# Two attention layers and two linear-attention layers on one core: another rule for TensorE's order, a one-product bias, and DMA transposes for the left-over rows

## The chip, the cores and the metric

The kernel runs on one core of a Trainium2 chip, in one launch. The time is the device time of one execution, in microseconds. A profile holds one execution, taken by the hardware profiler. Engines are TensorE (PE; its weight loads are listed as PEld), VectorE (DVE), ScalarE (ACT), GpSimd (POOL) and SyncE (SP), which here issues every DMA.

## The reference

Four blocks follow each other on x (1 x 2048 x 512): A, B, A, B, each added to its input after a layer norm.

```python
# A: 32 heads of 128, 8 memory rows, segments of 32 rows, one after the other
for s in range(n_seg):
    h = concat([mem, xs])                    # 8 + 32 = 40 rows
    q, k, v = h @ Wq, h @ Wk, h @ Wv
    p = softmax(where(mask, q @ k.T * scale, -1e9))
    o = (p @ v) @ Wo
    mem = o[:, :8]                           # feeds the next segment
    outs.append(o[:, 8:])
# B: 32 heads of 16, linear attention
pq, pk = phi(q), phi(k)                      # phi(t) = where(t > 0, t + 1, exp(t)) + 1e-6
o = (pq @ (pk.T @ v)) / (pq @ sum(pk) + 1e-6)
out = o @ wo
```

The mask lets every row see the 8 memory rows, and a row of the segment see the rows up to its own. A block of type A has 64 segments in a chain: the memory that leaves one segment enters the next.

## The kernel before, in words

All weights of A lie in SBUF from the start: Wq, Wk, Wv (512 x 4096) and Wo, 4 MB each. Working buffers lie in one tile, the arena, which A and B layers use in turn.

**How a segment is tiled.** The 40 rows of a segment are cut: a block of 32 rows holds the 8 memory rows and the segment's first 24 rows. The last 8 rows of four segments together make one more block of 32 rows, the left-over block of a group of four (`left_block`), and it doesn't depend on the memory. `project` multiplies a block by a weight: the block's 32 rows are the stationary side, so four matmuls stand side by side in TensorE's columns (tile form 128 x 32), each with 512 columns of the weight, four heads at once; four rounds over the 512 inputs. One PSUM bank then holds 16 heads (`b` is the half of the heads) in the layout "rows x head width". Values are used like that. Queries and keys are needed the other way round: `transposed` copies the bank to an image in SBUF (`img`, four slots), makes four transposes on TensorE (line 646, tile form 128 x 128) and copies the result to `qT` or `kT`, for the left-over block to `qTl` or `kTl`.

**The chain of a segment.** `mem_attention` (the memory's 8 queries against all 40 rows) starts its PSUM bank with a bias, the product of two constant tables `u16` and `w16` (line 701; 16 rows and 2 x 128 columns, tile form 16 x 128), adds the scores (710), takes the exponential (717), the sums (722), and the products with the values (735, 736), which are normalised into `oTb` (739). `out_block` multiplies by Wo (808, tile form 128 x 32 again) into `outW`, and `next_mem` brings the 8 memory rows back to the next segment's block (827). `x_attention` does the other 32 rows of the segment (759 scores, 763 exponential, 771 and 772 sums, 774 to 782, 792 and 793 values) and has until the next segment's `out_block`. `residual` adds the result to x (842, 847, 850). `prepare` makes the layer norm and the left-over block of the next group.

**What sets the order.** Nothing is issued as the functions are written. `P.add` records each operation with its cost, what it reads and writes, and its PSUM tile. `P.schedule`, once for each layer, walks a planned clock of each engine and picks, among the operations that are ready at that time, the one with the longest planned path to the layer's end (`tail`). Copies out of PSUM may go to ACT or DVE, whichever is planned to end first. For TensorE there are two further rules. Operations have a `mode` (`full`, `col` for the tile form 128 x 32, `bias`); among ready ones PE takes one of the mode that it is in, as long as its tail is at most MODE_SLACK (0.3) shorter than the longest. And a PSUM tile that isn't urgent starts only while three of the eight banks are free. Each engine then executes its own list in that order, and waits on semaphores for the others.

**B layers.** For each of 16 row tiles: layer norm, the three projections (914, 921), phi (898 to 901), the sums over all rows (937); then for each tile the numerator and denominator (956, 962), the quotient (967 to 971), transposes (979), the output projection (988) and the addition to x (991). Their two weights are loaded when the A layer has ended.

Of the kernel before, what the change touches and what calls it, by code (L numbers as in the profile page):

```python
# [18 lines left out]
MODE_SLACK = 0.3  # L19
# [35 lines left out]
class _Node:  # L55
    __slots__ = ("engs", "fn", "cost", "sync", "order", "tiles", "dsem", "dval", "eng", "start", "done",
                 "tail", "sig", "val", "waits", "know", "idx", "succ", "nleft", "urgent", "mode")


class _Prog:  # L60
# [17 lines left out]
    def add(self, engs, fn, cost, reads=(), writes=(), tiles=(), dsem=None, urgent=False, mode="full",  # L78
            after=()):
        nd = _Node()  # L80
        nd.mode = mode
        nd.engs = (engs,) if isinstance(engs, str) else tuple(engs)
# [41 lines left out]
    def schedule(self):  # L124
# [15 lines left out]
        for nd in reversed(nodes):  # L140
# [6 lines left out]
            nd.tail = best + min(nd.cost.values())  # L147
# [13 lines left out]
        n_left = len(nodes)  # L161
        pend = {e: [] for e in ENGINES}
# [25 lines left out]
        def n_free(t_now):  # L188
            k = 0
            for own in self.bank_owner:  # L190
                if own is None or (own.ops[-1].done is not None and own.ops[-1].done <= t_now):
                    k += 1
            return k
# [3 lines left out]
        def pick_for(e):  # L197
            tn = self.now[e]
            while pend[e] and pend[e][0][0] <= tn + EPS:
                _, _, nd = heapq.heappop(pend[e])  # L200
                if nd.done is None:
                    heapq.heappush(ready[e], (-nd.tail, nd.idx, nd))
            pick = None
            kept = []
            while ready[e]:
# [4 lines left out]
                if first_of(nd):  # L210
                    bf = bank_for(tn)
                    if bf is None or bf[1] > tn + EPS or (not nd.urgent and n_free(tn) < 3):
                        kept.append(item)
                        continue
# [10 lines left out]
                elif nd.tail < pick.tail - MODE_SLACK:  # L225
# [12 lines left out]
        while n_left:  # L238
# [47 lines left out]
            nd.done = nd.start + nd.cost[e]  # L286
            self.now[e] = nd.done - (0.09 if e == "act" else 0.05 if e == "dve" else 0.0)
# [94 lines left out]
def _build_kernel(nc, A_x, A_mem0, A_Wq, A_Wk, A_Wv, A_Wo, A_seg_len, B_wqkv, B_wo, out):  # L382
# [35 lines left out]
    w16_sb = sb("w16_sb", [128, 4, 2, 32])  # L418
# [31 lines left out]
    img = av(NI * 512).rearrange("p (r x) -> p r x", r=NI)  # L450
# [14 lines left out]
    xlnA = av(D).rearrange("p (r x) -> p r x", r=1)  # L465

# [73 lines left out]

    BIG = -1.0e9
    pool(lambda g: g.memset(w16_sb[:, :, 0, :], 0.0), ["w16"])
    pool(lambda g: g.memset(w16_sb[:, :, 1, :], BIG), ["w16"])
    for gg in range(4):
        a = w16_sb[:, gg, 0, :]
        sel(a, GE, BIG, 0, [[-4, 4], [0, 8]], 1, "w16")
        sel(a, GE, BIG, 3, [[4, 4], [0, 8]], -1, "w16")
        sel(w16_sb[:, gg, 1, :], ALU.not_equal, 0.0, -gg, [[-4, 4], [0, 8]], 1, "w16")
# [71 lines left out]
    def a_layer(layer):  # L620
        img_no = [0]
# [14 lines left out]
        def transposed(W, key, blk, bkeys, b, dst, dkey, urgent):  # L636

            tl = project(W, key, blk, bkeys, b, urgent)
            k = img_no[0] % NI
            img_no[0] += 1  # L640
# [11 lines left out]

        def left_block(G):
# [3 lines left out]
            for b in range(2):  # L657
                hs = slice(4 * b, 4 * b + 4)
                transposed(Wq_sb, "Wq", blk, bk, b, qTl[:, r2, hs, :, :], ("qTl", r2, b), False)
# [385 lines left out]
```

## Time and profile before

| | |
|---|---|
| runs, median (lowest to highest) | 2161.87 us (2161.3 to 2163.71) |
| profiled execution, its own time | 2159.93 us |
| mean granted TensorE clock | 0.994 |
| line 630, projections: matmuls | 15360 |
| line 808, output projection: matmuls | 5184 |
| ACT, copies out of PSUM and others on line 498 | 673.2 us in 1410 |
| DVE, the same on line 499 | 312.3 us in 541 (casts), 205.8 us in 543 (copies) |
| HBM over the span | 12 GB/s |

Times are in microseconds, of one entry in nanoseconds. "PE" is the engine's matmuls, "PEld" the loads of stationary tiles, which overlap them. A row of the order of time begins with the start and the duration of a run of like instructions; in brackets stands the idle time before it on its engine and what ended it. A matmul's end is modelled and overlaps the next one's start, so on TensorE the distance from start to start is the time that something takes. A stretch's row has its bounds, its length, and for each engine the busy time and the number of instructions, then the granted clock, the DMA engines' share and their GB/s.

### The profile page before, as it was taken

The numbers are of one execution on the slowest core, as the hardware profiler recorded it, in microseconds if no ns is written. First come the engines' busy times: TensorE is split into PE (matmuls) and PEld (weight loads), VectorE is DVE, ScalarE is ACT, GpSimd is POOL, SyncE is SP. The second block draws the span as 40 slices with busy tenths as digits, with TensorE's granted clock in tenths as the row PEclk, the third lists the DMA queues.
The fourth block names the chain that finished last, engine by engine and source line by source line (L and its number), as shares of the span: only waits on it lengthen the run. The fifth ranks groups of instructions, "written<-read, shape, count | busy, mean of one in ns | idle before, by whom it ended". The sixth has DMA issues, their size and how long they took to land.

```text
span 2158.2 us, 83024 instructions
## 1 busy us (share of the span) xinstructions
PE 2079.3 (96%) x37982; PEld 1163.5 (54%) x37982; DVE 1201.2 (56%) x3287; ACT 1159.7 (54%) x3112; POOL 14.8 (1%) x74
## 2 busy tenths in 40 slices
PE   1999999999999999998999999999999999999989
PEld 0555555555555555554655555555555555555545
DVE  0655555555554555556876555555555555554678
ACT  0555555555555555554645555555555555555554
POOL 2000000000000000000000000000000000000000
PEclk9999999999999999999999999999999999999999
DMA  9000000000000000001000000000000000000011
GB/s 350 3 3 2 3 3 3 3 3 3 3 3 3 3 3 3 3 3 41 1 2 3 3 3 3 3 2 3 3 3 3 3 3 3 3 3 3 3 41 40
DMA packets 12558, 30.48 MB, mean 14 GB/s; under 512 B 424, under 2 KB 9648, under 8 KB 10672
## 3 DMA queue, kind: packets, MB, share of 16 engines
q1 hardware_dynamic: 12208, 25.18, 3.2%
q8 instruction: 297, 4.87, 0.9%
q14 instruction: 53, 0.43, 0.1%
HBM read 23.08 MB, written 2.10 MB: 12 GB/s over the span
## 4 chain that ended last, share of the span: by engine, by line
PE 94%; DVE 2%; DMA 2%; ACT 1%; issue 0%; SPq 0%
PE pb L630 42%; PE pb L808 14%; PE pb L646 8%; PE pb L792 4%; PE pb L827 3%; PE pb L921 3%; PE pb L710 3%; PE pb L701 3%; PE pb L842 2%; PE pb L722 2%; DMA x_sb<-in_A_x_dram 2%; PE pb L735 2%; PE pb L759 2%; PE pb L914 1%; PE pb L736 1%; PE pb L771 1%
## 5 line engine op out<-in xcount | busy, mean ns | idle before, releaser
L498 ACT ACTIVATE arena_sb<-pb 128x512 bf16<-128x512 f32 (+6 forms) x1410 | 673.2, 492 | 458.7 <-PE pb L630 269.7
L630 PE MATMUL pb<-Wq_sb,arena_sb 128*32 128x512 bf16 x5120 | 478.2, 383 | 0.9 <-ACT arena_sb L498 0.4
L630 PE MATMUL pb<-Wk_sb,arena_sb 128*32 128x512 bf16 x5120 | 472.5, 382 | 0.0
L499 DVE CAST arena_sb<-pb 128x512 bf16<-128x512 f32 (+2 forms) x541 | 312.3, 578 | 237.6 <-PE pb L793 142.5
L630 PE MATMUL pb<-Wv_sb,arena_sb 128*32 128x512 bf16 x5120 | 374.4, 383 | 0.0
L808 PE MATMUL pb<-Wo_sb,arena_sb 128*32 128x512 bf16 x5184 | 350.1, 381 | 0.0
L780 DVE TENSOR_TENSOR arena_sb<-arena_sb 32x256 bf16<-32x256 bf16 x512 | 213.3, 417 | 133.6 <-ACT arena_sb L776 121.7
L499 DVE COPY arena_sb<-pb 128x512 bf16<-128x512 bf16 (+1 forms) x543 | 205.8, 399 | 137.8 <-PE pb L646 134.3
L646 PE MATMUL pb<-id_sb,arena_sb 128*128 128x128 bf16 x2560 | 216.7, 220 | 0.0
L630 PEld LDWEIGHTS pb<-Wq_sb,arena_sb 128*32 128x32 bf16 x5120 | 134.4, 96 | 133.2 <-ACT arena_sb L498 14.6
L646 PEld LDWEIGHTS pb<-id_sb,arena_sb 128*128 128x128 bf16 x2560 | 145.0, 97 | 103.2 <-issue 41.6
L630 PEld LDWEIGHTS pb<-Wk_sb,arena_sb 128*32 128x32 bf16 x5120 | 134.6, 97 | 108.5 <-issue 2.5
L717 ACT ACTIVATE arena_sb<-pb 128x256 bf16<-128x256 f32 x256 | 97.5, 381 | 158.9 <-PE pb L710 158.8
L498 ACT ACTIVATE outW_sb<-pb 128x256 fp32r<-128x256 f32 x198 | 75.8, 383 | 195.9 <-PE pb L808 194.5
L808 PEld LDWEIGHTS pb<-Wo_sb,arena_sb 128*32 128x32 bf16 x5184 | 119.7, 95 | 102.4 <-issue 20.7
L630 PEld LDWEIGHTS pb<-Wv_sb,arena_sb 128*32 128x32 bf16 x5120 | 109.6, 95 | 76.9
L782 DVE TENSOR_TENSOR arena_sb<-arena_sb 32x64 bf16<-32x64 bf16 x512 | 111.0, 217 | 15.8
L792 PE MATMUL pb<-arena_sb 128*128 128x128 bf16 x1024 | 115.2, 218 | 4.0 <-DVE arena_sb L782 4.0
L710 PE MATMUL pb<-arena_sb 128*128 128x32 bf16 x2048 | 118.6, 177 | 0.0
L499 DVE COPY arena_sb<-arena_sb 128x128 bf16<-128x128 bf16 x192 | 35.9, 194 | 128.8 <-PE pb L759 127.8
L793 PE MATMUL pb<-arena_sb 128*128 128x32 bf16 x1024 | 105.6, 178 | 0.0
L827 PEld LDWEIGHTS pb<-selm_sb,outW_sb 128*128 128x128 f32 x504 | 77.6, 188 | 51.8 <-ACT outW_sb L498 18.2
(108 smaller groups left out, 2330.6 us busy)
## 6 DMA issues: line engine op xcount, KB each, us to landing
Wq_sb<-in_A_Wq_dram SPq DMA_DIRECT2D x1, 4096.0 KB, 12.4
Wk_sb<-in_A_Wk_dram SPq DMA_DIRECT2D x1, 4096.0 KB, 22.2
Wv_sb<-in_A_Wv_dram SPq DMA_DIRECT2D x1, 4096.0 KB, 31.7
Wo_sb<-in_A_Wo_dram SPq DMA_DIRECT2D x1, 4096.0 KB, 43.2
arena_sb<-in_B_wqkv_dram SPq DMA_DIRECT2D x2, 1536.0 KB, 6.5
out_dram<-x_sb SPq DMA_DIRECT2D x16, 128.0 KB, 1.7
x_sb<-in_A_x_dram SPq DMA_DIRECT2D x1, 1920.0 KB, 11.5
arena_sb<-in_B_wo_dram SPq DMA_DIRECT2D x2, 512.0 KB, 7.5
```

The lines of the kernel that those rows point to most:

```text
L498: return e.activation(o() if callable(o) else o, i() if callable(i) else i, ACTF.Copy)
L499: return e.tensor_copy(o() if callable(o) else o, i() if callable(i) else i)
L630: r = pe.matmul(tl.f32()[32 * j:32 * j + 32, 0:512], blk[:, c, :], W[:, c, o:o + 512], start=(c == 0), stop=(c == 3), tile_position=(0, 32 ...
L646: r = pe.transpose(tt.bf16()[:, 128 * i:128 * i + 128], img[:, k, 128 * i:128 * i + 128], id_sb[:, :])
L710: r = pe.matmul(tl.f32()[:, o:o + 32], kk[:, hh, :, :].rearrange("p j x -> p (j x)"), qT[:, r2, hh, :, 0:8], start=False, stop=True, skip_ ...
L717: add("act", lambda a: a.activation(Pm[:, k, :, :].rearrange("p a q -> p (a q)"), tl.f32()[:, 0:256], ACTF.Exp, scale=SCALE), c_act(256), ...
L780: add("dve", lambda v, q=q, j=j: v.tensor_tensor(Pbx[q, :, j, 0:32], Px[q, :, :], Rx[q, :, :], ALU.mult), c_dve(256), reads=["Px", "Rx"], ...
L782: add("dve", lambda v, q=q, j=j: v.tensor_tensor(Pbx[q, :, j, 32:40], PLL[q, g2, :, gl], Rx[q, :, 24:32], ALU.mult), c_dve(64), reads=[("P ...
L792: pe.matmul(o, vimg[:, r2, e], Pbx[:, hh, :, 0:32], start=True, stop=False)
L793: return pe.matmul(o[:, :, 24:32], vleft[:, g2, e], Pbx[:, hh, :, 32:40], start=False, stop=True)
L808: r = pe.matmul(tl.f32()[32 * j:32 * j + 32, :], oT[:, 4 * hh + j, :], Wo_sb[:, 8 * j + hh, :], start=(hh == 0), stop=(hh == 7), tile_posi ...
L827: r = pe.matmul(tl.f32()[:, 8 * c:8 * c + 8], outW[:, s % 3, 128 * c:128 * c + 128], selm_sb[:, :], start=True, stop=True)
```

## The change

Four things change together.

1. **The planner's rules.** MODE_SLACK goes from 0.3 to 2.0. The picking key becomes `prio`: the tail, raised to that of the matmul ahead of it on the same PSUM tile while that one is still to come. A PSUM tile may start when more than two banks are free, more than one if it is urgent, and any if it is the oldest that hasn't started; a bank counts as free only with the lag after its last reader. Planned costs of lines 827, 842 and 847 (of before) rise. An operation may have a latency `lat` beyond its engine's time.
2. **The bias.** One product over all 128 rows of `u16` and 256 columns takes the place of two over 16 rows; its rows beyond 16 are zero in `u16`. `w16` is four times as wide, lies in the arena, and is filled by GpSimd at the start of each A layer. The mode `bias` is gone.
3. **The left-over rows.** `left_block` calls `turned` for queries and keys: the projection and the copy to an image stay, and SP issues a DMA transpose from the image to `qTl` or `kTl`. The four transposes on TensorE and the copy out of PSUM behind them are gone. These images have two slots of their own (4 and 5).
4. **Line numbers.** 630 becomes 639, 646 655, 701 717, 710 725, 722 737, 735 and 736 750 and 751, 739 754, 759 774, 771 786, 792 and 793 807 and 808, 808 823, 827 842, 842 857, 498 and 499 516 and 517.

```diff
-MODE_SLACK = 0.3
+MODE_SLACK = 2.0
...
-            nd.tail = best + min(nd.cost.values())
+            nd.tail = best + min(nd.cost.values()) + nd.lat
+        for nd in nodes:
+            nd.prio = nd.tail
+            for tl in nd.tiles:
+                k = tl.ops.index(nd)
+                if k and tl.ops[k - 1] in nd.order and tl.ops[k - 1].done is None:
+                    nd.prio = max(nd.prio, tl.ops[k - 1].prio)
...
-                    if bf is None or bf[1] > tn + EPS or (not nd.urgent and n_free(tn) < 3):
+                    while tiles[oldest[0]].bank is not None:
+                        oldest[0] += 1
+                    spare = 0 if tiles[oldest[0]] in nd.tiles else 1 if nd.urgent else 2
+                    if bf is None or bf[1] > tn + EPS or n_free(tn + EPS) <= spare:
...
-                elif nd.tail < pick.tail - MODE_SLACK:
+                elif nd.prio < pick.prio - MODE_SLACK:
...
-    img = av(NI * 512).rearrange("p (r x) -> p r x", r=NI)
+    img = av((NI + 2) * 512).rearrange("p (r x) -> p r x", r=NI + 2)
...
+        def turned(W, key, blk, bkeys, b, dst, dkey):
+            tl = project(W, key, blk, bkeys, b, False)
+            k = NI + img_no[1] % 2
+            img_no[1] += 1
+            evac(img[:, k, :], lambda: tl.f32()[:, :], 512, tiles=[tl], writes=[("img", k)])
+            add("sp", lambda e: e.dma_start_transpose(dst.rearrange("p h j x -> p h (j x)"), img[:, k, :]), 0.1,
+                reads=[("img", k)], writes=[dkey], dsem="turn%d" % k, lat=3.0)
...
-                transposed(Wq_sb, "Wq", blk, bk, b, qTl[:, r2, hs, :, :], ("qTl", r2, b), False)
-                transposed(Wk_sb, "Wk", blk, bk, b, kTl[:, r2, hs, :, :], ("kTl", r2, b), False)
+                turned(Wq_sb, "Wq", blk, bk, b, qTl[:, r2, hs, :, :], ("qTl", r2, b))
+                turned(Wk_sb, "Wk", blk, bk, b, kTl[:, r2, hs, :, :], ("kTl", r2, b))
...
-            def bias(pe):
-                for a in range(2):
-                    r = pe.matmul(tl.f32()[:, 128 * a:128 * a + 128], u16_sb[0:16, :],
-                                  w16_sb[0:16, g, a, :].unsqueeze(1).to_broadcast([16, 4, 32]), start=(a == 0),
-                                  stop=False, skip_group_check=True)
-                return r
-            add("pe", bias, c_pe(2, 128), reads=["u16", "w16"], tiles=[tl], urgent=True, after=early, mode="bias")
+            add("pe", lambda pe: pe.matmul(tl.f32()[:, 0:256], u16_sb[:, :],
+                                           w16_sb[:, g, :, :, :].rearrange("p a h x -> p (a h x)"), start=True,
+                                           stop=False, skip_group_check=True),
+                c_pe(1, 256), reads=["u16", "w16"], tiles=[tl], urgent=True, after=early)
```

**Where the order moves.** Three places show it.

The first is PE in the steady state of an A layer, from the last keys of a segment on. Names are outputs and inputs, `pb` is PSUM, then the output's size; 32x512 and 32x32 are matmuls of the tile form 128 x 32. Before:

```order
L630 MATMUL pb<-Wk_sb,arena_sb 32x512 x16
L646 MATMUL pb<-id_sb,arena_sb 128x128 x8
L630 MATMUL pb<-Wq_sb,arena_sb 32x512 x4
L630 MATMUL pb<-Wv_sb,arena_sb 32x512 x12
L701 MATMUL pb<-w_sb,u_sb 128x128 x2
L646 MATMUL pb<-id_sb,arena_sb 128x128 x4
L710 MATMUL pb<-arena_sb 128x32 x8
L630 MATMUL pb<-Wv_sb,arena_sb 32x512 x4
L630 MATMUL pb<-Wk_sb,arena_sb 32x512 x4
L646 MATMUL pb<-id_sb,arena_sb 128x128 x4
L722 MATMUL pb<-arena_sb,one_sb 128x128 x2
L630 MATMUL pb<-Wq_sb,arena_sb 32x512 x4
```

and now, from the same place on:

```order
L639 MATMUL pb<-Wk_sb,arena_sb 32x512 x16
L639 MATMUL pb<-Wv_sb,arena_sb 32x512 x32
L655 MATMUL pb<-id_sb,arena_sb 128x128 x8
L717 MATMUL pb<-arena_sb,u_sb 128x256
L655 MATMUL pb<-id_sb,arena_sb 128x128 x8
L725 MATMUL pb<-arena_sb 128x32 x4
L717 MATMUL pb<-arena_sb,u_sb 128x256
L807 MATMUL pb<-arena_sb 128x128
L808 MATMUL pb<-arena_sb 128x4x8
L725 MATMUL pb<-arena_sb 128x32 x4
```

The values' projection stands in one piece ahead of the transposes, and the tile form changes once in the lower list and seven times in the upper one. Over the whole program it changes 2278 times before and 1228 times after, 34 and 14 of them in each stretch from the last segment's end of an A layer through the B layer behind it.

The second is SP's queue at the start. Before:

```order
L512 DMA Wq_sb<-in_A_Wq_dram 128x4x4096
L512 DMA Wk_sb<-in_A_Wk_dram 128x4x4096
L512 DMA Wv_sb<-in_A_Wv_dram 128x4x4096
L513 DMA Wo_sb<-in_A_Wo_dram 128x32x512
L509 DMA x_sb<-in_A_x_dram 128x512
L510 DMA arena_sb<-in_A_mem_dram 8x512
L514 DMA x_sb<-in_A_x_dram 128x15x512
```

and now:

```order
L530 DMA Wk_sb<-in_A_Wk_dram 128x4x4096
L530 DMA Wq_sb<-in_A_Wq_dram 128x4x4096
L527 DMA x_sb<-in_A_x_dram 128x512
L530 DMA Wv_sb<-in_A_Wv_dram 128x4x4096
L531 DMA Wo_sb<-in_A_Wo_dram 128x32x512
L668 DMA_TRANSPOSE arena_sb<-arena_sb 128x4x128
L528 DMA arena_sb<-in_A_mem_dram 8x512
L668 DMA_TRANSPOSE arena_sb<-arena_sb 128x4x128
L532 DMA x_sb<-in_A_x_dram 128x15x512
L668 DMA_TRANSPOSE arena_sb<-arena_sb 128x4x128 x62
```

The first tile of x comes ahead of Wv and Wo, the memory rows come behind the first transpose, and the rest of x behind the second; all transposes of the layer follow.

The third is ACT's list in the steady state of after, with the semaphores that each instruction waits for (`s_turn5` is the landing of a transpose from image slot 5):

```order
L742 ACTIVATE arena_sb<-arena_sb 128x128 [waits s_act]
L516 ACTIVATE arena_sb<-pb 128x512 [waits s_turn5,s_pe]
L516 ACTIVATE outW_sb<-pb 128x256 [waits s_pe]
L778 ACTIVATE arena_sb<-pb 128x256 [waits s_pe]
L516 ACTIVATE outW_sb<-pb 128x256 [waits s_act]
```

The second row is the copy of a left-over image into slot 5, which waits for the transpose that read the slot before; the evacuation of `outW`, which the next segment's memory needs, is queued behind it. Before, such a copy waited for PE alone.

49 lines of the change are left out of this document (28 added, 21 removed).

## The prediction

> **What bounds the kernel now.** I read the page first: the span, the engines' shares, the granted clock and the chain that ended last. Then the busy times by stage, then the order of time on TensorE.
>
> ```profile
> span 2158.2 us, 83024 instructions
> PE 2079.3 (96%) x37982; PEld 1163.5 (54%) x37982; DVE 1201.2 (56%) x3287; ACT 1159.7 (54%) x3112; POOL 14.8 (1%) x74
> PEclk9999999999999999999999999999999999999999
> PE 94%; DVE 2%; DMA 2%; ACT 1%; issue 0%; SPq 0%
> ```
>
> The profiled execution took 2159.93 us, the median of the three runs is 2161.87, so 1.9 us separate them. VectorE and ScalarE are a little over half busy and the clock is full. TensorE is on the chain for 94%. Its busy time alone proves little, because the ends of matmuls are modelled. The stages come next: stretch, length, then the busy time of PE, PEld, DVE, ACT, POOL.
>
> ```profile
> 49.00:992.00 943.00, 943.00 (x17899) 521.81 (x17899) 509.79 (x1413) 523.19 (x1424) 0.00 (x0) 1.00 0.01 3
> 992.00:1126.00 134.00, 117.86 (x1473) 71.25 (x1472) 102.08 (x260) 67.48 (x168) 0.21 (x2) 0.94 0.05 17
> ```
>
> The first stretch is the first A layer: PE has no gap in it. The second is the B layer with a segment at either end: there PE does wait (16 us). What PE does while "busy" is seen in the order of time, where the starts, not the ends, are to be read (start, duration, line):
>
> ```profile
> 502.36 1.04 PE L630 MATMUL pb<-Wq_sb,arena_sb 128*32 128x512 bf16 x16
> 503.22 1.04 PE L630 MATMUL pb<-Wk_sb,arena_sb 128*32 128x512 bf16 x16
> 504.19 0.62 PE L646 MATMUL pb<-id_sb,arena_sb 128*128 128x128 bf16 x8
> 504.74 0.40 PE L630 MATMUL pb<-Wq_sb,arena_sb 128*32 128x512 bf16 x4
> 504.97 0.82 PE L630 MATMUL pb<-Wv_sb,arena_sb 128*32 128x512 bf16 x12
> 505.73 0.28 PE L701 MATMUL pb<-w_sb,u_sb 16*128 16x128 bf16 x2
> 505.94 0.40 PE L646 MATMUL pb<-id_sb,arena_sb 128*128 128x128 bf16 x4
> 506.17 0.35 PE L710 MATMUL pb<-arena_sb 128*128 128x32 bf16 x8
> 506.46 0.40 PE L630 MATMUL pb<-Wv_sb,arena_sb 128*32 128x512 bf16 x4
> 506.68 0.39 PE L630 MATMUL pb<-Wk_sb,arena_sb 128*32 128x512 bf16 x4
> 507.00 0.40 PE L646 MATMUL pb<-id_sb,arena_sb 128*128 128x128 bf16 x4
> ```
>
> Sixteen column-tiled matmuls (128*32 weights, four side by side) take 503.22 - 502.36 = 0.86 us, so one group of four takes 0.215. Four transposes take 506.17 - 505.94 = 0.23, or 0.057 each, and the same 128*128 form follows them with no extra. Wherever the form changes there is an extra: 503.22 to 504.19 is 0.97 for 0.86 of work (0.11); 504.19 to 504.74 is 0.55 for 0.45 (0.10); 504.97 to 505.73 is 0.76 for 0.645 (0.11); 505.73 to 505.94, two products of the 16-row form, is 0.21 for 0.11 (0.10); 506.68 to 507.00 is 0.32 for 0.215 (0.10). **A change of tile form costs PE about 0.10 us**, and every start stands where the one before lets it. Counted over the whole program of before, the form changes 2278 times: 228 us.
>
> ```profile
> 514.73 0.76 PE L827 MATMUL pb<-selm_sb,outW_sb 128*128 128x8 f32 x4
> 574.62 0.75 PE L827 MATMUL pb<-selm_sb,outW_sb 128*128 128x8 f32 x4
> ```
>
> These two are the same matmul, four segments apart: 59.9 us. Adding up that stretch of the program at such intervals (0.215 a group, 0.057 a transpose, 0.026 for 32 columns and so on) gives 52.2 us of matmuls, and 72 changes at 0.10 add 7.2: 59.4. Real waiting is some 0.5 us in 60. So in the A layers time is TensorE's work plus its form changes.
>
> [...]
>
> **The change part by part.**
>
> *Form changes.* With MODE_SLACK 2.0, the wish to finish a tile, and a bias product of 128 rows in place of a 16-row form, the program of after changes form 1228 times: 1050 fewer, at 0.10 us **105 us**. All but 40 of them are in the A layers. The 40 are in the B layers, where PE waits anyway: I count their 4 us as not gained.
>
> *Transposes.* 2560 become 2048; 512 at 0.057 are **29 us** of PE. With them go 128 of these copies out of PSUM, 0.42 or 0.60 us each, on engines that are not the bound, so I count nothing for them:
>
> ```profile
> L646 PE MATMUL pb<-id_sb,arena_sb 128*128 128x128 bf16 x2560 | 216.7, 220 | 0.0
> L499 DVE COPY arena_sb<-pb 128x512 bf16<-128x512 bf16 x491 | 195.4, 420 | 136.0 <-PE pb L646 134.3
> L498 ACT ACTIVATE arena_sb<-pb 128x512 bf16<-128x512 bf16 x213 | 125.9, 597 | 41.3 <-PE pb L979 30.6 <-PE pb L646 10.8
> ```
>
> *Bias.* Two products of 128 columns (0.11) become one of 256:
>
> ```profile
> 499.95 0.28 PE L771 MATMUL pb<-arena_sb,bo_sb 128*128 128x256 bf16 x1
> 500.07 0.19 PE L772 MATMUL pb<-arena_sb,bo_sb 128*128 128x64 bf16 x1
> ```
>
> That is 0.12: no gain beyond the form changes already counted. Its table is now filled on GpSimd at each A layer's start, 14 instructions of 0.3 to 0.5 us by the rows below, some 5 us, while the first projections and transposes of that layer (about 10 us of PE work) run ahead of the first bias. Uncovered it would cost 5 us once.
>
> ```profile
> L524 POOL TENSOR_SCALAR_AFFINE_SELECT id_sb<-id_sb 128x128 bf16<-128x128 bf16 x1 | 0.3, 292 | 0.2 <-POOL id_sb L528 0.2
> L559 POOL MEMSET arena_sb<- 128x480 bf16 x1 | 0.5, 498 | 0.1
> ```
>
> *The DMA transposes.* 128 of them, 128 KB each, on SP, which does nothing else in an A layer. Each begins when its image has been copied from PSUM. In the steady state two kinds of instruction wait for one: the copy that refills the same image slot, and the copies and scores that read the result. Counting PE work between an image's last matmul and the waiting place, less the image's own copy (0.25 to start, 0.6 to run), the cover is about 3.4 us at three places in eight segments, about 4.5 at one, and 9 to 38 elsewhere: 48 and 16 places in the kernel. Behind the waiting copy on ACT stands the evacuation of outW, the recurrence itself. No row shows a DMA transpose. The nearest are
>
> ```profile
> out_dram<-x_sb SPq DMA_DIRECT2D x16, 128.0 KB, 1.7
> arena_sb<-in_B_wo_dram SPq DMA_DIRECT2D x2, 512.0 KB, 7.5
> ```
>
> Same size 1.7 us; the longest that does not queue behind the 16 MB of weights 7.5. I take the first, with room up to 3.4: **nothing**. At 7.5 it would be 48 x 4.1 + 16 x 3.0 = 245 us.
>
> [...]
>
> *Start.* SP's queue now has x's first tile third instead of fifth:
>
> ```profile
> 9.87 29.62 SPq L509 DMA_DIRECT2D x_sb<-in_A_x_dram  x1
> 45.96 0.69 DVE L601 BATCH_NORM_STATS2 st_sb<-x_sb 128x6 f32<-128x512 bf16 x1 [22.66 <-DMA x_sb<-in_A_x_dram]
> 48.48 0.26 PE L588 MATMUL pb<-id_sb,arena_sb 8*128 8x8 bf16 x4
> Wk_sb<-in_A_Wk_dram SPq DMA_DIRECT2D x1, 4096.0 KB, 22.2
> ```
>
> It waited 30 us for room behind Wo. Behind two weights it should land near 24 us, and the first left-over block (24 groups x 0.215 = 5.2 us) runs while Wv and Wo load. The first transpose now takes the blocked place and the memory rows (L588) follow it, so segment 0 begins near 47 to 50 us as now. I take **-6 us**, between +3 and -9.
>
> *New waits.* With PE's work shorter, the copies that it waits for have less to hide behind.
>
> ```profile
> 504.67 0.76 DVE L499 COPY arena_sb<-pb 128x512 bf16<-128x512 bf16 x2
> ```
>
> This copy starts 0.25 us after the first four of the transposes at 504.19 are through (504.42) and takes half of 0.76 when two follow each other, 0.42 alone: 0.67 us. In the order of after, between four L655 and the L725 that needs their copy stand four more (0.23), a bias (0.12) and eight (0.46): 0.81. Such places, with less than 0.1 us left once release and queue are counted, are some 18 in four segments, against some 11 before, and at one (L823 behind the product L754) about 0.4 us is missing. I take 1.1 us of waiting for four segments in place of 0.5, over 32 such stretches **+20 us**; from 0 to +105 (all the form changes given back).
>
> Sum: 2159.9 - 105 - 29 + 4 - 6 + 20 = 2044; with half of the difference to the median, **2045 us**.
>
> **Rivals.**
>
> 1. *A DMA transpose outlasts its cover.* For it: slot and reader wait in order, and 1.7 us is of a plain copy. Against: 3.4 us is twice that. At 4.2 us it costs 48 x 0.8 = 38 (2083), at 5 us 48 x 1.6 + 16 x 0.5 = 85 (2130).
> 2. *The same, beyond 5.5 us: slower than before.* There 48 x 2.1 + 16 x 1.0 = 117 eats the whole gain; at 6.5 us it is 48 x 3.1 + 16 x 2.0 = 181, 2225 us. ACT's idle 46% could soften it, since not all of its delay reaches PE.
> 3. *The longer runs of one form starve the recurrence.* Copies wait longer for a whole tile, and the saved changes come back as gaps before L655, L725 and L842: half gives 2097, all 2150. Against: 0.5 us of waits in 60 now, and a chain through one segment of some 10 us by the same rows (16 groups 3.4, transposes and copies 1.5, exponential to product 2, output projection 0.9 to 1.7, two copies and L827 1.2) under 13.8 us of PE work for one.
> 4. *PE is not the bound*, so nothing changes: 2155 to 2160. The starts speak against it.
>
> That the change doesn't do what it says is excluded by the counts of its program, all but the price of 0.10.
>
> **How the numbers follow.** Forecast (2020 to 2070) 0.61, rival 1 0.18, rival 3 0.09, rival 2 0.09, rival 4 0.03. A measurement of this kernel can tell 0.2%, 4 us. Faster by more: 0.61 + 0.18 + 0.09 = 0.88; within it 0.03; slower 0.09. The range goes from 2020 (no new waits, the full start) to 2110: it leaves out rivals 2 and 4 and the upper ends of 1 and 3, some 0.05 and 0.03.
>
> **What would show it.** Four segments should take 55 to 57 us from L842 to L842; PE gaps in the A layers should be where L725, L737 and L823 wait for copies. DMA transposes should land within 3.4 us of issue, and no ACT or DVE copy should wait long for one; if such waits stand first in the list of waits, rival 1 or 2 is right. If the extra at a change of form is not 0.10 in the new trace, the main term is wrong. PE's first layer-norm transpose should start near 26 us.

## The result, and the profile after

| | before | after |
|---|---|---|
| median of 4 runs each, one chip (lowest to highest) | 2161.59 us (2160.55 to 2163.71) | 2032.28 us (2029.36 to 2033.56) |
| ratio, with its 95% interval | | 0.9399 [0.9382, 0.9415] |
| profiled execution, its own time | 2159.93 us | 2032.45 us |

The change takes 129 us off, 13 more than forecast. The page of after, first the span, the engines' shares and the granted clock, then the chain that ended last:

```profile
span 2030.7 us, 81374 instructions
PE 1946.7 (96%) x37214; PEld 1150.5 (57%) x37214; DVE 1015.3 (50%) x3068; ACT 1274.8 (63%) x3203; POOL 23.6 (1%) x88
PEclk8999999999999999998999999999999999999989
PE 93%; DMA 2%; DVE 2%; ACT 1%; issue 0%; SPq 0%; DVEq 0%
```

TensorE is the bound as before, with the same 96%: the span became shorter because TensorE has less to do, and not because it waits less (outside its busy time there are 79 us of the span before and 84 after). VectorE became idler and ScalarE busier, as the planner gives ScalarE more of the copies; in the chain they have 2% and 1%, as before.

Next the two stretches that answer to those of before: the first A layer, and the B layer between the last `next_mem` of one A layer and the first of the next (bounds, length, busy time of each engine, granted clock, DMA share, GB/s).

```profile
66.00:910.00 844.00, 839.50 (x16873) 494.20 (x16863) 402.46 (x1256) 555.27 (x1403) 0.00 (x0) 1.00 0.07 12
923.70:1059.00 135.30, 117.55 (x1460) 71.47 (x1460) 95.78 (x249) 70.19 (x172) 6.17 (x16) 0.92 0.09 21
```

PE now has 4.5 us of gaps in 844 where it had none in 943. Through the B layer it idles 17.8 us of 135.3, before 16.1 of 134.0: little changed, as the bias and the left-over rows are work of the A layers. The granted clock there is 0.92, before 0.94.

The order of time on PE gives the pace. The last matmul group of `next_mem` at the same place, eight segments apart, and rows with and without a change of form between them:

```profile
483.20 1.90 PE L639 MATMUL pb<-Wv_sb,arena_sb 128*32 128x512 bf16 x32
485.04 0.62 PE L655 MATMUL pb<-id_sb,arena_sb 128*128 128x128 bf16 x8
485.49 0.27 PE L717 MATMUL pb<-arena_sb,u_sb 128*128 128x256 bf16 x1
485.60 0.61 PE L655 MATMUL pb<-id_sb,arena_sb 128*128 128x128 bf16 x8
492.11 0.38 PE L842 MATMUL pb<-selm_sb,outW_sb 128*128 128x8 f32 x2
602.20 0.82 PE L639 MATMUL pb<-Wv_sb,arena_sb 128*32 128x512 bf16 x12
602.95 0.39 PE L842 MATMUL pb<-selm_sb,outW_sb 128*128 128x8 f32 x2
603.60 0.39 PE L842 MATMUL pb<-selm_sb,outW_sb 128*128 128x8 f32 x2
```

From 492.11 to 603.60 are 111.5 us for eight segments, 55.7 for four; before it was 59.9. From 483.20 to 485.04 is 1.84 us for eight groups of 0.215 (1.72): the change of form costs 0.12. From 602.20 to 602.95 is 0.75 for 0.645: 0.10. Between L655, L717 and L655 there is nothing extra: the new bias product has the form of the transposes around it.

What PE still waits for, from the list of waits (instruction, what released it, us in total, times, longest), and the two waits of it that matter here in the order of time:

```profile
PE pb L623 <- DVE arena_sb L616: 38.2, 4, 26.3
PE pb L597 <- DMA arena_sb<-in_A_mem_dram: 11.7, 1, 11.7
PE pb L823 <- DVE arena_sb L754: 8.3, 17, 0.6
PE pb L737 <- ACT arena_sb L732: 2.0, 3, 0.9
...
26.33 0.61 PE L623 MATMUL pb<-id_sb,arena_sb 128*128 128x128 bf16 x4 [26.33 <-DVE arena_sb L616]
47.98 0.27 PE L597 MATMUL pb<-id_sb,arena_sb 8*128 8x8 bf16 x4 [11.73 <-DMA arena_sb<-in_A_mem_dram]
475.29 0.62 PE L823 MATMUL pb<-Wo_sb,arena_sb 128*32 128x512 bf16 x8 [0.51 <-DVE arena_sb L754]
```

The first row is the start and the layer changes. The second is new: the load of the memory rows stands behind the first DMA transpose in SP's queue, and that behind Wo's bytes. The third is the only wait of the steady state with a size: the output projection behind the product L754, 17 times in 128 segments. Two of the page's groups (busy time, mean ns of one, idle time before) show that neither the transposes nor the memory queries' scores (L725) ever stand idle:

```profile
L725 PE MATMUL pb<-arena_sb 128*128 128x32 bf16 x2048 | 102.8, 177 | 0.0
L655 PE MATMUL pb<-id_sb,arena_sb 128*128 128x128 bf16 x2048 | 157.3, 219 | 0.0
```

The DMA transposes, as the view of their source line has them (durations in ns are SP's, the last line is from issue to landing):

```profile
L668 SPq DMA_TRANSPOSE arena_sb<-arena_sb x128: 1189/1190/12458, 30.0 to 1879.0; - x128
  DVE arena_sb L517: 36.3, 17
  ACT arena_sb L516: 12.2, 13
  PE pb L688: 0.6, 2
DMA to landing us min/median/max: 2.4/2.5/17.6
```

They take 1.19 us to issue and 2.5 us to land, 17.6 only behind the weights at the start. VectorE's and ScalarE's copies wait for them 30 times; PE itself waits 0.6 us in the whole program.

Where the 127.5 us between the two spans lie, by marks in the trace (the last L842, L827 before, of the first and of the last segment of each A layer): up to the first 6.7 less (63.98 us against 70.69), first A layer 61.5 less (859.7 against 921.2), through the first B layer 1.1 more (135.3 against 134.2), second A layer 62.1 less, last B layer 1.7 more. (The two stretches behind the A layers' last marks are called B parts below.) Between its marks each A layer of after leaves PE some 5 us of gaps, 10.7 in all, where before has none:

```profile
63.98:923.65 859.67, 853.95 (x17146) 503.05 (x17146) 410.73 (x1282) 564.91 (x1427) 0.00 (x0) 1.00 0.07 12
1058.98:1918.00 859.02, 853.99 (x17148) 503.42 (x17148) 411.99 (x1286) 565.95 (x1428) 0.00 (x0) 1.00 0.07 12
```

### The profile page after: what moved, and what is told of

Read it like the earlier page. It is cut to its first block, busy times and chain, and to the rows that moved or that the text cites. A ratio compares the mean times of both kernels' runs of the same rounds, so it can differ in the third digit from the quotient of the medians.

```text
span 2030.7 us, 81374 instructions
## 1 busy us (share of the span) xinstructions
PE 1946.7 (96%) x37214; PEld 1150.5 (57%) x37214; DVE 1015.3 (50%) x3068; ACT 1274.8 (63%) x3203; POOL 23.6 (1%) x88
## 4 chain that ended last, share of the span: by engine, by line
PE 93%; DMA 2%; DVE 2%; ACT 1%; issue 0%; SPq 0%; DVEq 0%
PE pb L639 43%; PE pb L823 15%; PE pb L655 6%; PE pb L842 3%; PE pb L807 3%; PE pb L944 3%; PE pb L725 3%; PE pb L857 2%; PE pb L737 2%; DMA Wv_sb<-in_A_Wv_dram 2%; PE pb L717 2%; PE pb L774 2%; PE pb L1011 1%; PE pb L937 1%; PE pb L750 1%; PE pb L751 1%
## 5 line engine op out<-in xcount | busy, mean ns | idle before, releaser
L516 ACT ACTIVATE arena_sb<-pb 128x512 bf16<-128x512 f32 (+6 forms) x1535 | 796.0, 523 | 421.9 <-PE pb L639 275.7
L639 PE MATMUL pb<-Wk_sb,arena_sb 128*32 128x512 bf16 x5120 | 353.3, 384 | 0.8 <-ACT arena_sb L516 0.8
L823 PE MATMUL pb<-Wo_sb,arena_sb 128*32 128x512 bf16 x5184 | 337.1, 384 | 8.7 <-DVE arena_sb L754 8.3
L639 PE MATMUL pb<-Wq_sb,arena_sb 128*32 128x512 bf16 x5120 | 344.4, 383 | 0.5 <-ACT arena_sb L516 0.5
L517 DVE COPY arena_sb<-pb 128x512 bf16<-128x512 bf16 (+2 forms) x474 | 178.5, 405 | 311.1 <-PE pb L655 307.4
L639 PE MATMUL pb<-Wv_sb,arena_sb 128*32 128x512 bf16 x5120 | 323.5, 380 | 0.5 <-DMA Wv_sb<-in_A_Wv_dram 0.5
L517 DVE CAST arena_sb<-pb 128x128 bf16<-128x128 f32 (+3 forms) x357 | 132.7, 375 | 179.6 <-PE pb L808 64.0
L639 PEld LDWEIGHTS pb<-Wv_sb,arena_sb 128*32 128x32 bf16 x5120 | 130.6, 96 | 121.7 <-DMA Wv_sb<-in_A_Wv_dram 0.6
L823 PEld LDWEIGHTS pb<-Wo_sb,arena_sb 128*32 128x32 bf16 x5184 | 122.1, 96 | 120.8 <-issue 11.3
L655 PE MATMUL pb<-id_sb,arena_sb 128*128 128x128 bf16 x2048 | 157.3, 219 | 0.0
L655 PEld LDWEIGHTS pb<-id_sb,arena_sb 128*128 128x128 bf16 x2048 | 122.6, 97 | 55.4 <-ACT arena_sb L516 54.4
L842 PEld LDWEIGHTS pb<-selm_sb,outW_sb 128*128 128x128 f32 x504 | 75.1, 188 | 64.8 <-ACT arena_sb L778 23.8
L725 PE MATMUL pb<-arena_sb 128*128 128x32 bf16 x2048 | 102.8, 177 | 0.0
L517 DVE CAST outW_sb<-pb 128x256 fp32r<-128x256 f32 x105 | 44.5, 424 | 106.5 <-ACT outW_sb L516 103.4
```

The costliest lines, as they stand in the source:

```text
L516: return e.activation(o() if callable(o) else o, i() if callable(i) else i, ACTF.Copy)
L517: return e.tensor_copy(o() if callable(o) else o, i() if callable(i) else i)
L639: r = pe.matmul(tl.f32()[32 * j:32 * j + 32, 0:512], blk[:, c, :], W[:, c, o:o + 512], start=(c == 0), stop=(c == 3), tile_position=(0, 32 ...
L655: r = pe.transpose(tt.bf16()[:, 128 * i:128 * i + 128], img[:, k, 128 * i:128 * i + 128], id_sb[:, :])
L725: r = pe.matmul(tl.f32()[:, o:o + 32], kk[:, hh, :, :].rearrange("p j x -> p (j x)"), qT[:, r2, hh, :, 0:8], start=False, stop=True, skip_ ...
L823: r = pe.matmul(tl.f32()[32 * j:32 * j + 32, :], oT[:, 4 * hh + j, :], Wo_sb[:, 8 * j + hh, :], start=(hh == 0), stop=(hh == 7), tile_posi ...
```

## The experiments

Twelve kernels ran in three groups, each group beside the kernel before on its own chip (2162.06, 2161.34 and 2162.09 us there). All times are medians of four runs, of seven for these three.

| run | us (lowest to highest) | ratio to before, 95% interval | form changes |
|---|---|---|---|
| after | 2032.28 (2029.36 to 2033.56) | 0.9399 [0.9382, 0.9415] | 1228 |
| after, bias as two products | 2074.75 (2074.45 to 2075.07) | 0.9596 [0.9581, 0.961] | 1680 |
| before, slack 2 and the rule for banks | 2136.81 (2135.72 to 2139.61) | 0.9885 [0.987, 0.9899] | 1818 |
| before, new bias | 2138.8 (2138.01 to 2139.51) | 0.9893 [0.9876, 0.9909] | 2014 |
| before, DMA transposes | 2127.45 (2126.33 to 2128.64) | 0.9839 [0.9825, 0.9854] | 2193 |
| after, transposes on PE | 2072.61 (2071.99 to 2073.07) | 0.959 [0.9576, 0.9605] | 1322 |
| after, slack 0.3 | 2063.24 (2062.93 to 2063.73) | 0.9548 [0.9532, 0.9564] | 1586 |
| after, each DMA transpose twice | 2135.97 (2127.93 to 2139.75) | 0.9879 [0.9858, 0.99] | 1228 |
| after, start reordered | 2043.94 (2042.43 to 2047.02) | 0.946 [0.9446, 0.9474] | 1230 |
| after, slack 8 | 2025.65 (2023.49 to 2026.97) | 0.9366 [0.935, 0.9381] | 1104 |
| after, memory rows first | 2037.79 (2037.29 to 2039.57) | 0.9427 [0.9413, 0.9441] | 1230 |
| after, memory rows first, slack 8 | 2039.45 (2038.19 to 2040.21) | 0.9432 [0.9418, 0.9446] | 1120 |
| after, memory rows first, Wo late | 2037.7 (2036.54 to 2039.78) | 0.9426 [0.9412, 0.944] | 1236 |

### The price of a change of form, by itself

The bias of after is made as two products of 16 rows again, at the same places in the order, with the same planned cost:

```diff
-            add("pe", lambda pe: pe.matmul(tl.f32()[:, 0:256], u16_sb[:, :],
-                                           w16_sb[:, g, :, :, :].rearrange("p a h x -> p (a h x)"), start=True,
...
+            def bias(pe):
+                for a in range(2):
+                    r = pe.matmul(tl.f32()[:, 128 * a:128 * a + 128], u16_sb[0:16, :],
+                                  w16_sb[0:16, g, a, :, :].rearrange("p h x -> p (h x)"), start=(a == 0),
...
+            add("pe", bias, c_pe(1, 256), reads=["u16", "w16"], tiles=[tl], urgent=True, after=early)
```

> The changed kernel with the bias again as two products of 16 rows and 128 columns, put by the planner at the very same places (its cost and mode left as they are), so that only the number of form changes differs: 1680 against 1228. If a form change costs PE 0.10 us and PE is the bound: 452 x 0.10 = 45 us more, 2032 + 45 = 2077. If PE had room and the changes were hidden: 2032. If a form change cost 0.05: 2055.

42.5 us more for 452 more changes: **0.094 us each** (0.090 to 0.101 by the lowest and highest runs of both kernels). Between the marks the traces have 438 of the changes in the two A layers, which became 43.1 us longer: 0.098 each. The columns streamed are the same, and so is the time of two short products, as the order of time shows:

```profile
496.24 0.28 PE L719 MATMUL pb<-arena_sb,u_sb 16*128 16x128 bf16 x2
496.46 0.62 PE L655 MATMUL pb<-id_sb,arena_sb 128*128 128x128 bf16 x8
```

From 496.24 to 496.46 are 0.22 us, 0.11 beside one change of form, as the one long product of after takes (485.49 to 485.60). So nothing but the form is left to explain the difference.

### One part at a time on the kernel before

Two of the rules alone, `MODE_SLACK` and the rule for banks. The expectation speaks of three, but this kernel's edit leaves out `prio`, the wish to finish a tile, and the raised planned costs; no run has these by themselves:

```diff
-MODE_SLACK = 0.3
+MODE_SLACK = 2.0
...
-                    if bf is None or bf[1] > tn + EPS or (not nd.urgent and n_free(tn) < 3):
+                    while tiles[oldest[0]].bank is not None:
+                        oldest[0] += 1
+                    spare = 0 if tiles[oldest[0]] in nd.tiles else 1 if nd.urgent else 2
+                    if bf is None or bf[1] > tn + EPS or n_free(tn + EPS) <= spare:
```

> The kernel before with the planner's three rules alone (slack 2.0, finish a tile first, the bank rule): 1818 form changes against 2278, transposes and bias as before. Theory (PE's work plus 0.10 for each change): 460 x 0.10 = 46 us less, 2161.6 - 46 = 2115. Rival (longer runs of one form starve the recurrence): half of that given back, 2138 or more.

25 us less, where 460 fewer changes at 0.094 make 43: what the rival had said, about half of it is given back. Most of the 18 us are found as gaps of PE. In the two A layers they come to 12.9 us, where the kernel before has none; the list of waits names the larger part (its L818 is the output projection, L745 the first of the memory queries' products with the values):

```profile
PE pb L818 <- DVE arena_sb L749: 5.6, 27, 0.4
PE pb L745 <- ACT arena_sb L508: 5.2, 30, 0.2
```

Neither of these stands among the kernel before's waits. They are 10.8 us. By the marks the two B parts are 1.6 and 2.0 us longer besides.

The bias alone:

```diff
-            add("pe", bias, c_pe(2, 128), reads=["u16", "w16"], tiles=[tl], urgent=True, after=early, mode="bias")
+            add("pe", lambda pe: pe.matmul(tl.f32()[:, 0:256], u16_sb[:, :],
...
+                c_pe(1, 256), reads=["u16", "w16"], tiles=[tl], urgent=True, after=early)
```

> The kernel before with the one-product bias alone: 2014 form changes against 2278. Theory: 264 x 0.10 = 26 us less, 2135. Rival: the bias was hidden behind copies, 2158 to 2162.

23 us less, for 264 changes: 25 at 0.094.

The DMA transposes alone (with the new rule for banks, slack 0.3):

```diff
-                transposed(Wq_sb, "Wq", blk, bk, b, qTl[:, r2, hs, :, :], ("qTl", r2, b), False)
-                transposed(Wk_sb, "Wk", blk, bk, b, kTl[:, r2, hs, :, :], ("kTl", r2, b), False)
+                turned(Wq_sb, "Wq", blk, bk, b, qTl[:, r2, hs, :, :], ("qTl", r2, b))
+                turned(Wk_sb, "Wk", blk, bk, b, kTl[:, r2, hs, :, :], ("kTl", r2, b))
```

> The kernel before with the DMA transposes, and the bank rule that the planner needs to find an order with them; slack 0.3, no finishing rule, two-product bias. 2193 form changes against 2278 and 512 transposes fewer. Theory: 85 x 0.10 + 29 = 37 us less, and 6.7 from the earlier start (the first tile of x comes third in the queue here too), 2118. Rival (its gain lies in the copies that ACT and DVE no longer make): more than that, 2090 or less; rival (transposes on PE were cheap fill): 2150.

34.6 us less, 9.6 fewer than the 44 expected; PE has 7.3 us of gaps in its two A layers, where the kernel before has none. The three parts add up to 83 us, and the whole change gives 129. 23 us of the difference are counted: together they remove 1050 changes, one by one 460 + 264 + 85 = 809. Why cannot be told from these runs: the rule for banks is in two of the three kernels, `prio` and the raised costs in none, and the rules may find longer runs once the bias and the left-over transposes no longer break them up.

### One part taken out of the kernel after

The transposes back on TensorE (the last diff the other way round):

> The changed kernel with the left-over rows' queries and keys transposed on TensorE again, from their own two image slots: 1322 form changes against 1228, 512 transposes more, and the first tile of x back in fifth place. Theory: 94 x 0.10 + 29 + 6.7 = 45 us more, 2077. Rival (the DMA transposes save nothing, PE's transposes were cheap fill): 2035 to 2040.

40.3 us more. 512 transposes are 29, 94 changes 8.8, and the first mark is at 68.4 us in place of 64.0, 4.4: 42.

The slack back to 0.3, all else as in after:

```diff
-MODE_SLACK = 2.0
+MODE_SLACK = 0.3
```

> The changed kernel with MODE_SLACK back at 0.3: 1586 form changes against 1228. Theory: 358 x 0.10 = 36 us more, 2068. Rival (the longer runs cost waits that the shorter ones don't): 2032 to 2050.

31 us more, for 358 changes: 33.7 at 0.094.

### How much later a DMA transpose may land

Each transpose is made twice, the second after the first has landed, and readers wait for the second:

```diff
+            def twice(e):
+                P.xn = getattr(P, "xn", 0) + 16
+                e.dma_start_transpose(dst.rearrange("p h j x -> p h (j x)"), img[:, k, :]).then_inc(P.sems["turnx"], 16)
+                e.wait_ge(P.sems["turnx"], P.xn)
+                return e.dma_start_transpose(dst.rearrange("p h j x -> p h (j x)"), img[:, k, :])
...
-            add("sp", lambda e: e.dma_start_transpose(dst.rearrange("p h j x -> p h (j x)"), img[:, k, :]), 0.1,
+            add("sp", twice, 0.1,
```

> The changed kernel with every DMA transpose made twice: SP waits for the first to land and issues the second, whose landing releases what waits. Same order on every engine; issue to landing about 5 us where it was 2.5. By the prediction's price for a landing of 5 us, 48 places x 1.6 + 16 x 0.5 = 85 us more at most: 2117. If ACT's and DVE's idle time takes up most of a late landing: 2035 to 2060. If no cover is ever short: 2032.

104 us more, above the 85 that the first rival was priced at. In the order of time of this kernel, on SP's queue, ScalarE and PE, one such place:

```profile
605.19 1.20 SPq L670 DMA_TRANSPOSE arena_sb<-arena_sb  x1
609.32 1.19 SPq L672 DMA_TRANSPOSE arena_sb<-arena_sb  x1
612.48 1.19 SPq L670 DMA_TRANSPOSE arena_sb<-arena_sb  x1
614.90 1.26 SPq L672 DMA_TRANSPOSE arena_sb<-arena_sb  x1
...
611.85 0.60 ACT L516 ACTIVATE arena_sb<-pb 128x512 bf16<-128x512 f32 x1 [3.62 <-DMA arena_sb<-arena_sb]
...
612.50 1.05 PE L639 MATMUL pb<-Wq_sb,arena_sb 128*32 128x512 bf16 x16 [1.09 <-ACT arena_sb L516]
```

The pair issued at 612.48 and 614.90 lands 2.5 us after the second, 4.9 us after the first. The pair before it took longer, 6.6 us until 611.8, and held ScalarE's copy into the image slot for 3.62 us, behind which PE stood idle for 1.09. So the mechanism of the first rival exists, at the place that it named, and the landing of 2.5 us is what keeps it shut. By the marks (L848 here) the two A layers are 49 and 45 us longer, the start 10, the two B parts 3. The A layers between their marks:

```profile
74.35:983.43 909.08, 872.88 (x17147) 506.88 (x17146) 408.39 (x1281) 560.74 (x1427) 0.00 (x0) 0.98 0.11 20
1119.91:2023.71 903.80, 870.50 (x17149) 506.23 (x17148) 409.81 (x1286) 561.46 (x1428) 0.00 (x0) 0.99 0.12 20
```

PE's gaps went from 10.7 us to 69.5, which is 59 of the 94 us. The other 35 are the same matmuls, which keep PE busy for longer at a granted clock of 0.98 and 0.99 in place of 1.00. In the lists of waits:

```profile
ACT arena_sb L516 <- DMA arena_sb<-arena_sb: 103.2, 38, 3.7
DVE arena_sb L517 <- DMA arena_sb<-arena_sb: 143.0, 45, 20.5
PE pb L694 <- DMA arena_sb<-arena_sb: 25.4, 13, 3.4
```

The third row is a wait that the first rival had not priced: PE itself, at the left-over rows' scores (L694 here, L688 in after), with everything behind it.

### Longer runs still

```diff
-MODE_SLACK = 2.0
+MODE_SLACK = 8.0
```

> The changed kernel with runs of one tile form allowed to be 8 us late instead of 2 us: 1104 form changes instead of 1228. Theory (TensorE bound, 0.094 us per form change as the first of these runs gave): 124 x 0.094 = 11.7 us less, 2020.6 us. Rival (longer runs starve the recurrence, the third of the prediction): the gain is eaten by TensorE's waits behind the recurrence's VectorE and ScalarE steps; 2032 us or more, with more and longer waits at L725, L737 and L823.

6.6 us less, and the fastest kernel of the study: its four runs lie below all four of after. By the marks the A layers are 6.9 and 2.5 us shorter, the B parts behind them 0.8 and 2.9 longer, the start 0.3. Of the 11.7 expected, 9.4 arrives in the A layers. The waits at L823 shrink, and another comes up beside them, for the copies of the left-over rows' output:

```profile
PE pb L862 <- ACT outWl_sb L516: 6.3, 29, 0.5
PE pb L823 <- DVE arena_sb L754: 2.0, 6, 0.6
```

### The start, four attempts

After's 11.7 us wait at L597 invited a repair. The first attempt moved three loads: the memory rows to the front of SP's queue, Wo behind the first four transposes, the rest of x behind Wo.

```diff
-    add("sp", lambda s: s.dma_start(mem0_sb[0:M, :], A_mem0[0]), 2.0, writes=[MEM0], dsem="dmem")
+    add("sp", lambda s: s.dma_start(mem0_sb[0:M, :], A_mem0[0]), 2.0, writes=[MEM0], dsem="dmem", lat=60.0)
...
-    add("sp", lambda s: s.dma_start(Wo_sb[:, :, :], A_Wo.rearrange("h e d -> e h d")), 12.0, writes=["Wo"], dsem="dWo")
-    add("sp", lambda s: s.dma_start(x_sb[:, 1:NT, :], x_view[:, 1:NT, :]), 6.0,
-        writes=[("x", t) for t in range(1, NT)], dsem="dx1")
...
+            wo = add("sp", lambda s: s.dma_start(Wo_sb[:, :, :], A_Wo.rearrange("h e d -> e h d")), 12.0, writes=["Wo"],
+                dsem="dWo", after=turns[:4])
+            add("sp", lambda s: s.dma_start(x_sb[:, 1:NT, :], x_view[:, 1:NT, :]), 6.0,
+                writes=[("x", t) for t in range(1, NT)], dsem="dx1", after=[wo])
```

> The changed kernel with another start: the memory rows first in SP's queue, Wo behind the first block's four transposes, the rest of x behind Wo. The changed kernel's PE waits 11.8 us for the memory rows. Theory (that wait is the start's own loss, and what then binds is Wo at about 50 us, needed by the first output projection): 6 to 10 us less, 2022 to 2026. Rival (the load of 16 MB binds either way): 2030 to 2033.

It lost 12 us. Its order of time has a gap on PE (L653 is the transposes' line there) between two halves of the first segment's transposes. ScalarE's copy for them was queued behind the layer norm of a later tile, and that waited on VectorE for the rest of x, which this edit put behind Wo:

```profile
64.85 0.69 DVE L607 BATCH_NORM_STATS2 st_sb<-x_sb 128x6 f32<-128x512 bf16 x1 [22.47 <-DMA x_sb<-in_A_x_dram]
...
66.64 0.61 PE L653 MATMUL pb<-id_sb,arena_sb 128*128 128x128 bf16 x4 [15.43 <-ACT arena_sb L516]
```

Three further kernels take the moves apart. The memory rows first, and nothing else moved (the first pair of lines of the diff above):

> The changed kernel with the load of the memory rows first in SP's queue instead of behind the first transpose; nothing else is moved (1230 form changes). It separates the two changes made at the start in the run before, which lost 12 us. Theory: TensorE's 11.7 us wait at L597 goes, the next thing that is late there is the first transposed tile, behind Wo's load: between 0 and 11.7 us less, 8 taken, 2024 us; the loss of the run before came from the rest of x issued behind Wo. Rival: the loss came from the memory rows' new place or from what TensorE does in place of the wait: 2035 us or more.

5.5 us slower than after: both the theory and its bound of 0 fail, and the rival's 2035 or more holds. The wait did go from L597, and PE stands at two others instead:

```profile
47.41 0.30 PE L688 MATMUL pb<-arena_sb 128*32 128x32 bf16 x16 [11.00 <-DMA arena_sb<-arena_sb]
56.43 0.61 PE L623 MATMUL pb<-id_sb,arena_sb 128*128 128x128 bf16 x4 [8.72 <-DVE arena_sb L616]
...
59.34 0.26 PE L597 MATMUL pb<-id_sb,arena_sb 8*128 8x8 bf16 x4
```

The edit did more than move a load. `lat=60.0` gives the load a long tail, so that it is issued first, and it also makes the planner believe that the rows land at 2 + 60 = 62 us. In after it plans them at 52.1 (by the planned costs in the queue, 12 + 12 + 2 + 12 + 12 + 0.1, and 2 for the load). So the planner put the left-over scores (L688) and the next tile's layer norm (L623) ahead of the memory rows, and those wait for the first DMA transpose behind Wo's bytes and for the rest of x. The memory rows, whose load now stands first in the queue, come to PE only at 59.34. The first mark is at 74.0 us in place of 64.0: 10.0 later, where the plan for the rows moved by 9.9. That the plan is the cause is read from the order and was not tested by itself. Half of that is made up later: the first A layer is 1.8 us shorter than after's, and the B part behind it 2.9, at a granted clock of 0.96 in place of 0.92. All four attempts carry this `lat`; a load that comes early and is planned early was not run.

The same with Wo's load behind the first four transposes, and the rest of x still ahead of it:

```diff
+            turns.append(nd)
...
+        if layer == 0:
+            add("sp", lambda s: s.dma_start(Wo_sb[:, :, :], A_Wo.rearrange("h e d -> e h d")), 12.0, writes=["Wo"],
+                dsem="dWo", after=turns[:4])
```

> The changed kernel with the memory rows first and Wo's load behind the first four transposes, the rest of x still ahead of Wo (1236 form changes). It keeps Wo's move from the start experiment that lost 12 us and takes back the move of x. Theory (the rest of x was the loss): SyncE no longer stands 12.5 us and 16 us behind Wo's packets at the first transposes, the first segment starts earlier, and Wo is needed only at the first L823: 2 to 12 us less than the changed kernel, 2025 us taken. Rival (Wo's being late was the loss): 2040 us or more, with TensorE waiting at L823 for Wo.

2037.7 against 2037.79: on the whole Wo's place is worth nothing, and neither the theory (at most 2030) nor the rival (2040 or more) holds. By the marks the first one comes 4.3 us earlier (69.7 for 74.0), and the first A layer and the B part behind it take 2.4 and 4.0 us more, the B part at a granted clock of 0.91 in place of 0.96. So of the first attempt's 11.7 us, 5.5 belong to the memory rows' edit, its `lat` included, and 6.2 to the rest of x behind Wo. The 12.5 us that the expectation gives SyncE behind Wo are the issue of after's first transpose (12.46 us; here the first two take 2.70). Its 16 us are not such a wait: they are a row of three transposes, the first at 49.25 and the third at 64.19, and Wo has landed by 46.8.

Memory rows first and slack 8 together:

> Both of the two edits before: memory rows first and runs up to 8 us late, 1120 form changes instead of 1228. Theory: both gains add, 108 x 0.094 = 10.2 us and 8 us at the start: 2014 us. Rival: they share one wait, so that the sum is no better than the better of the two.

No better than with slack 2, where slack 8 on after's own start gave 6.6: by the marks the A layers are 2.5 and 2.3 us shorter than with slack 2, and the two B parts 4.3 and 2.6 longer. The first of these goes with the clock. These are its stretches, with slack 2 and with slack 8:

```profile
931.87:1064.29 132.42, 112.65 (x1448) 70.03 (x1460) 95.83 (x249) 70.14 (x172) 6.17 (x16) 0.96 0.08 21
929.92:1066.64 136.72, 116.44 (x1447) 71.83 (x1460) 96.20 (x249) 70.47 (x172) 6.16 (x16) 0.93 0.08 21
```

The same work keeps PE busy for 3.8 us more at a granted clock of 0.93 in place of 0.96. The last B part has 0.94 in both; its 2.6 us stay open.

## Why the prediction was right

*TensorE's work is the bound* (rival 4 excluded). The pace of 55.7 us for four segments lies in the 55 to 57 that the prediction named. Three kernels that only changed the number of forms moved by 0.09 us a change: 452, 264 and 358 changes by 0.094, 0.088 and 0.086 each. Two others gained about half of that, 25 us for 460 changes and 6.6 for 124; there PE's gaps or the B parts took some of it back. The busy share of the weight loads doesn't tell the bound here: it is 57% in after, and the span still follows the matmuls' starts.

*Form changes, 105 us.* Right: 0.094 to 0.098 us were measured for 0.10. The prediction put 40 of the changes in the B layers. In the traces the stretch from the last mark of the first A layer to the first of the second goes from 34 to 14, but the one from the second A layer's last mark to the program's end only from 14 to 6; the A layers lose 1018, which are 96 to 100 us. The changes in the B parts brought nothing, as priced; those parts even became 2.8 us longer, at a lower granted clock (0.92 for 0.94 in the first, 0.94 for 0.97 in the last).

*Transposes, 29 us.* Right: 40.3 us when they go back to TensorE, of which 13 are form changes and start.

*Bias.* No gain beyond its form changes: 23 us alone for 25 counted.

*DMA transposes, nothing.* Right, on a thinner cover than thought. The landing taken from the plain copy of the same size was 1.7 us; it is 2.5, against 3.4 of cover. At twice that, the first rival's loss is there, and larger than its price (104 for 85): PE's own wait at the left-over scores (25.4 us there), the start (10) and the lower clock (0.98 and 0.99 for 1.00) were not in that price.

*Start, -6 us.* 6.7. PE's first layer-norm transpose was put near 26 us and came at 26.33. That the memory rows' load goes behind the blocked transpose was in the step; that PE would stand idle for 11.7 us there was not. Four attempts did not cure it, all of them with the memory rows planned at 62 us; whether an early load that is planned early would, stays open.

*New waits, +20 us.* **This term was mis-sized.** The A layers became 123.6 us shorter, where the prediction has 105 - 4 + 29 - 20 = 110. 1018 changes at 0.094 to 0.098 and 512 transposes at 0.057 are 125 to 129, which leaves 1 to 5 us for new waits; the gaps of PE are 10.7 us, of which 8.3 stand in the list at L823, the place that was named. So the term was between 1 and 11. The step counted places with under 0.1 us left and took a wait at each; at L725 PE idles 0.0 us, so those copies are in time. This term is nearly the whole 13 us by which the forecast lay above the result; the 2.8 us by which the B parts became longer, where the prediction had nothing, hid a little of it by luck.

*Longer runs starve the recurrence* (rival 3). Not at slack 2 in the changed kernel: going from 0.3 to 2.0 gave 31 of 33.7 us. It is visible on the kernel before, where slack and the rule for banks without `prio` gave 25 of 43, and at slack 8, where a part of the gain comes back as waits elsewhere.

## What to carry to other kernels

Where TensorE is the bound, read it from start to start and count how often the tile form changes: each change cost 0.094 us here, and an order that groups like forms, or an operand padded to the neighbours' form, gives that back without touching the arithmetic. Work moved to an idle DMA queue cost TensorE 0.6 us of direct waits here at a landing of 2.5 us, and 104 us of the kernel's time when each transfer was made twice: measure the cover in that way before you count on it. When a planner sets the order, an edit that moves a load can move everything that is planned to wait for it: compare the plan's times for that load before and after, and test the two apart.

## What the runs showed of the hardware

**After the 11.73 us wait of after's start, TensorE worked at half its clock for some 5 us.** These stretches of after are the wait for the memory rows and what follows it (columns as above, the granted clock is third from last):

```profile
36.00:48.00 12.00, 0.27 (x9) 0.03 (x2) 0.00 (x0) 0.63 (x2) 0.00 (x0) 0.65 1.16 302
48.00:52.20 4.20, 3.65 (x40) 1.42 (x44) 0.79 (x2) 1.51 (x4) 0.00 (x0) 0.50 1.10 348
52.20:56.00 3.80, 3.80 (x64) 1.68 (x60) 0.88 (x2) 2.40 (x5) 0.00 (x0) 0.85 0.54 142
56.00:64.00 8.00, 7.73 (x188) 4.91 (x180) 6.86 (x21) 7.11 (x27) 0.00 (x0) 1.00 0.02 5
```

PE's last matmul ahead of the wait ended at 36.25 (47.98 less 11.73). In stretches of 0.2 us the granted clock is 1.00 until 39.6, 0.78 to 39.8 and 0.50 behind that, so it fell at about 39.7, 3.5 us after that end. It is 0.50 for the 4.2 us after the wait, still 0.50 from 53.0 to 53.2, 0.59 to 53.4 and 1.00 behind that, so it rose at about 53.4, 5.4 us after PE took up work. The kernel with the memory rows first shows the like: behind its waits of 11.00 and 8.72 us the clock is 0.55 from 57.4 to 62.4 and 1.00 from there. Going by the clock, after's wait cost more than its own length, by some 2.7 us (an estimate, half of the 5.4).

**Each DMA transpose made 544 packets of under 512 B.** Before had 12558 packets in all, 424 of them under 512 B; after has

```profile
DMA packets 82184, 47.17 MB, mean 23 GB/s; under 512 B 70056, under 2 KB 79280, under 8 KB 80304
```

which is 544 more for each of the 128, by either count, and with every transpose made twice there are 151817, 544 more again.
